# A convolution's first stage in three products of column halves, with its intermediate laid out for runs of 4 KB

## The chip, the cores and the metric

The kernel runs on one core of one Trainium2 chip. The metric is the device time of one execution in microseconds (us), the median of several runs. A core has TensorE (PE; PEld is its loading of weights), VectorE (DVE), ScalarE (ACT), GpSimd (POOL) and SyncE (SP), which issues nearly all transfers here. The data move on 16 DMA engines that all transfers share.

## What is computed

The reference is a long convolution by FFT, followed by a "soft" mixture of experts over the convolution's rows, all in float32:

```
x (8, 5696, 128), h (5696, 128)
y = irfft(rfft(x, 2S) * rfft(h, 2S))[:, :S]          # causal convolution along the sequence
t = y.reshape(45568, 128)
logits = t @ phi                                     # phi (128, 32): 8 experts x 4 slots
slots  = softmax(logits, over tokens).T @ t          # (32, 128)
out    = softmax(logits, over slots) @ expert_mlp(slots)    # 1024 hidden units, relu
```

The convolution is done as a transform of 90 x 64 points (`N1 = 90`, `N2 = 64`; 89 rows of 64 tokens hold the 5696 tokens), forward for `h` and the eight batches of `x`, a product with `h`'s transform, and back.

## The kernel before

The work is software-pipelined by hand: a loop over steps `t` issues a piece of each stage, and the order of the instructions on each engine's queue is the order in which the loop writes them. There are 72 steps with a first stage (`NA = 72`: `h` and eight batches, eight chunks each), then ten steps without it (`without_a`), then a tail.

**First stage, one chunk a step.** `load_x(c)` (L178) loads 89 rows into one of three buffers, as a transfer of 80 rows and one of 9. `fold(c, comp)` (L195) makes, on POOL, the sum (`comp` 0) and the difference (`comp` 1) of two mirrored column blocks, 128 x 512 each, into `xf[comp]`. `stage_a(c, comp)` (L204) multiplies one fold by two 128-column tables (L211), evacuates each product on ACT (L213) into `fst`, and stores the useful rows into the DRAM tensor `fd[g]` of shape (2, 64, 45, 2, 128): half of the frequencies `a`, position `n2`, frequency `q`, part `c`, channel. Each store has 45 rows and four runs of 1 KB in a row (L217). There are two a call, four a chunk. `stage_a(t, 0)` opens a step and `stage_a(t, 1)` stands after `stage_c5`, in the step's later half.

**Second stage, three units a step (23 a batch).** `load_g(u)` (L224) loads two frequencies of all 128 pairs (a, n2) as one run of 2 KB per row (L230), four units ahead, into five buffers `gt`. `stage_b1` multiplies (L244, PSUM tile `bt`) and applies `h`'s transform on DVE (L265, L268, L270). `stage_b2` multiplies again (L284), evacuates into `zst` on ACT (L288) and stores it into the DRAM tensor `zd` (L289). A step has three places for this, `slot_b`. It begins at `t = 9` (`LAG_B`). The group `g = 0`, the transform of `h`, only fills tables.

**Third stage and the mixture, one pair of chunks in two steps,** from `t = 27` (`LAG_C`), with loads two steps ahead. `load_pair` (L308) loads from `zd` into the one buffer `zc` in two transfers, of 64 and of 26 rows of 16 KB. `stage_c1` multiplies (L336: each product is two matmuls of 64 columns whose results stand in the two halves of a PSUM bank), `after` (L353) adds on DVE (L341, L342) and POOL (L359). `stage_c2` to `stage_c6`, `softmax` and `dispatch` transpose, take logits and exponentials, and accumulate the slots. `stage_c6` stores the token softmax into DRAM (`c_t`).

**The tail** computes the last batch's third stage, joins the four partial maxima (`join_quarters`), runs the experts and writes the output (L860 to L877). The last store (L875) has 128 rows in SBUF that go to 8 batches x 16 rows in DRAM.

SP issues the transfers in program order, and one that waits holds up all behind it.

Of the kernel before, what the change touches and what calls it, by code (L numbers as in the profile page):

```python
# [10 lines left out]
F32 = mybir.dt.float32  # L11
AF = mybir.ActivationFunctionType
AL = mybir.AluOpType
# [6 lines left out]
    return [(0, 64, 32), (64, n - 64, 0)]  # L20


def transform_tables(S, N1, N2, CH, X0, F0, F1):

    N, R1, HALF, P = N1 * N2, S // N2, N2 // 2, 2 * N2
    k1 = np.arange(N1)
    alpha = np.pi * (k1 + 0.5) / N1
    m1 = np.arange(R1) - (N1 - 1) / 2
    a1 = np.outer(m1, alpha)  # L40
    s1 = np.stack([np.cos(a1), -np.sin(a1), -np.cos(a1)], 1)
    a0 = np.outer(alpha, np.arange(N1 // 2) + 0.5)
    i1 = np.stack([np.cos(a0), -np.sin(a0), -np.cos(a0)], 1)
    NP = N1 // 2
    part = s1
    s1 = np.zeros((P, 3, P))
    for a, p in enumerate((F0, F1)):
        s1[X0:X0 + R1, :, p:p + NP] = part[:, :, a * NP:(a + 1) * NP]
    part = i1[np.arange(N1).reshape(2, NP).T.reshape(-1)]
    i1 = np.zeros((P, 3, N2))  # L50
    for r, n, p in z_blocks(N1):
        i1[p:p + n, :, 0:NP] = part[r:r + n]
    k2 = np.arange(N2)
    omega = np.pi * (k1[:, None] + 2 * N1 * k2[None] + 0.5) / N
    m2 = np.arange(HALF) - (N2 - 1) / 2
    a2 = m2[None, :, None] * omega[:, None, :]
    w = np.concatenate([np.cos(a2), np.sin(a2)], 1)
    back = np.arange(N2).reshape(2, HALF // CH, CH).transpose(1, 0, 2).reshape(-1)
    NU = (NP + 1) // 2
    turn = (N1 - 1) / 2 * alpha[:, None] + (N2 - 1) / 2 * omega  # L60
    wq = np.zeros((2, N2, NP, N2))
    vq = np.zeros((2, N2, NU, 2, N2))
    tn = np.zeros((2, N2, 2, NU, 2))
    for a in range(2):
        wq[a] = w[a * NP:(a + 1) * NP].transpose(1, 0, 2)
        for q in range(NP):
            vq[q % 2, :, q // 2, a] = w[a * NP + q][back].T
            tn[q % 2, :, 0, q // 2, a] = np.cos(turn[a * NP + q]) / N
            tn[q % 2, :, 1, q // 2, a] = np.sin(turn[a * NP + q]) / N
    wq, vq, tn = [t.reshape(P, *t.shape[2:]) for t in (wq, vq, tn)]  # L70
    return [np.ascontiguousarray(t, dtype=np.float32) for t in (s1, i1, wq, vq, tn)]
# [3 lines left out]
def kernel(  # L75
# [33 lines left out]
    CH = 4  # L109
# [6 lines left out]
    NQ = NJ // 2  # L116
    assert S == R1 * N2 and R1 == N1 - 1 and D == P and CH == Q == 4
    SPLIT = R1 // 16 * 16
    X0, F0, F1 = 20, 6, 82
    ctx.enter_context(tc.manual_schedule())  # L120

    t_s1, t_i1, t_w, t_v, t_turn = [
        nc.inline_tensor(t, f"tab_{n}").ap()
        for n, t in zip(("s1", "i1", "w", "v", "turn"), transform_tables(S, N1, N2, CH, X0, F0, F1))]
    fd = [nc.dram_tensor(f"f_{g}", (2, N2, NP, 2, D), F32, kind="Internal").ap() for g in range(B + 1)]
    zd = [nc.dram_tensor(f"z_{b}", (NP, 2 * N2, 2, D), F32, kind="Internal").ap() for b in range(B)]
    cd = nc.dram_tensor("c_t", (P, B * NQ, Q, 2, MH), F32, kind="Internal").ap()

# [28 lines left out]
    apool = lead.enter_context(tc.tile_pool(name="apool", bufs=2, side="right"))  # L157
    bpool = front.enter_context(tc.tile_pool(name="bpool", bufs=1))

    s1 = apool.tile([P, 3, P], F32, name="s1", tag="s1", bufs=1)  # L160
    wt = fconst.tile([P, NP, HP], F32, name="wt")
    vt = fconst.tile([P, NU, 2, HP], F32, name="vt")
    turn = fconst.tile([P, 2, NU, 2], F32, name="turn")
# [6 lines left out]


    xs = {}
    xf = [apool.tile([P, CH, D], F32, name=f"x{i}", tag=f"x{i}", bufs=1) for i in range(2)]
    xcs = [apool.tile([P, 2, CH, D], F32, name=f"xc{i}", tag=f"xc{i}", bufs=1) for i in range(3)]
    for t_ in xcs:
        nc.vector.memset(t_[:, :, :, :], 0.0)
# [18 lines left out]
    def fold(c, comp):  # L195
        if c not in xs:
            return
        t_ = xs.pop(c) if comp else xs[c]
        y_ = xf[comp]
        nc.gpsimd.tensor_tensor(out=y_[:, :, :], in0=t_[:, 0, :, :], in1=t_[:, 1, ::-1, :],  # L200
                                op=AL.subtract if comp else AL.add)
        folded[(c, comp)] = y_

    def stage_a(c, comp):  # L204
        g, j = divmod(c, NJ)
        src = folded.pop((c, comp))
        tab = (0, 1) if comp == 0 else (1, 2)
        st = apool.tile([P, CH, 2, D], F32, name="fst", tag="fst", bufs=3)
        for G in range(2):
            p = bank()  # L210
            nc.tensor.matmul(p[:, :], s1[:, tab[G], :],  # L211
                             src[:, :, :].rearrange("p n d -> p (n d)"), start=True, stop=True)
            nc.scalar.activation(st[:, :, G, :],  # L213
                                 p[:, :].rearrange("p (n d) -> p n d", d=D), AF.Copy)
        n0 = comp * HALF + CH * j
        for a, p in enumerate((F0, F1)):
            nc.sync.dma_start(  # L217
                out=fd[g][a, n0:n0 + CH, :, :, :].rearrange("n q c d -> q n (c d)"),
                in_=st[p:p + NP, :, :, :].rearrange("k n c d -> k n (c d)"))


    gs, prods = {}, {}
# [1 line left out]
    def load_g(u):  # L224
        if u >= (B + 1) * NU:
            return
        g, i = divmod(u, NU)
        n = min(2, NP - 2 * i)
        t_ = bpool.tile([P, 2, 2, D], F32, name="gt", tag="gt", bufs=5)
        nc.sync.dma_start(  # L230
            out=t_[:, 0:n, :, :].rearrange("p q c d -> p (q c d)"),
            in_=fd[g].rearrange("a r q c d -> (a r) (q c d)")[:, 4 * i * D:(4 * i + 2 * n) * D])
        gs[u] = t_

    def stage_b1(u, adder=nc.vector):
# [88 lines left out]
    def stage_c1(T):  # L324
# [27 lines left out]

        def after(a_):  # L353
            fold_out(a_, om[:, :, :], op[:, :, :])

            def additions():
                for v, o_, eng in ((1, op, nc.gpsimd), (0, om, nc.vector if tail else nc.gpsimd)):
                    for part_, sign in ((part(v, 1), AL.subtract), (part(v, 0), AL.add)):
                        eng.tensor_tensor(out=part_, in0=part(v, 0), in1=o_[:, :, :], op=sign)  # L359
            return additions  # L360

        ys[T] = y_
        return second
# [140 lines left out]
    def join_quarters():  # L504
# [5 lines left out]
        nc.vector.tensor_reduce(out=lr[:, 0, :], in_=p[0:1, 0:P].rearrange("p (k s) -> p s k", k=Q),  # L510
                                axis=AX.X, op=AL.min)
        nc.vector.tensor_copy(out=lr[:, 1:Q, :], in_=lr[:, 0:1, :].broadcast_to([1, Q - 1, NSL]))

        def spread():
            p = bank()
            nc.tensor.matmul(p[:, 0:1], lr[:, :, :].rearrange("p k s -> p (k s)"), one[:, :],
                             start=True, stop=True)
            le = tail["last"].tile([P, 1], F32, name="le")
            nc.vector.tensor_tensor(out=le[:, :], in0=p[:, 0:1], in1=low[:, 1:2], op=AL.subtract)
            nc.scalar.activation(le[:, :], le[:, :], AF.Exp)  # L520
            once = tail["last"].tile([P, NSL], F32, name="once")
            nc.vector.tensor_scalar(out=once[:, :], in0=rep4[:, 0, :], scalar1=le[:, 0:1],
                                    scalar2=None, op0=AL.mult)
            tail["once"] = once
        return spread


    LAG_B, LAG_C = NJ + 1, 3 * NJ + 3
# [13 lines left out]
    loaded = 0  # L542

    load_x(0)
    nc.scalar.dma_start(out=s1[:, :, :], in_=t_s1)
    for c in range(1, 3):
        load_x(c)
    nc.sync.dma_start(out=wt[:, :, :], in_=t_w)
# [8 lines left out]
    for t in range(last_front + 1):  # L557
# [35 lines left out]
        def without_a():  # L593
# [7 lines left out]
            if T is not None:  # L601
# [4 lines left out]
                    add(kept_[0])  # L606
                slot_around(middle, nc.gpsimd)
                load_pair(pair(-2))
                additions = kept_[1]()
                slot_around(lambda: stage_c5(U), nc.gpsimd)  # L610
                additions()
                softmax(U)
                return
            if t == last_front:
                load_pair(V + 2, (0,))
            slot_around(lambda: dispatch(pair(3)), nc.vector)
            slot_around(lambda: stage_c2(V, (3, 2)), nc.vector)
            slot_around(lambda: stage_c2(V, (1, 0)), nc.gpsimd)
            assert t < last_front or not (us or wait_b2)
            if t == last_front:  # L620
# [17 lines left out]
        if t >= NA:  # L638
            without_a()
            continue  # L640
        stage_a(t, 0)
        fold(t + 1, 0)
        if t == NA - 1:
            stage_a(t, 1)
        if pair(3) is not None:
            dispatch(pair(3))
        slot_b()
# [10 lines left out]
        if pair(5) is not None:  # L658
            stage_c6(pair(5))
        slot_b()  # L660
        if pair(-2) is not None:
            load_pair(pair(-2))
        load_x(t + 3)
        if t == NJ:
            prefetch(AHEAD)
        if after:
            after()()
        if U is not None:
            stage_c5(U)
        if t < NA - 1:  # L670
            stage_a(t, 1)
            fold(t + 1, 1)
        if pair(1) is not None:
            stage_c3(pair(1))
        slot_b()
# [19 lines left out]

    second = stage_c1(T)
    stage_c4(T - 1)
    second()()()
    stage_c5(T - 1)
    softmax(T - 1)  # L700
    nc.gpsimd.memset(y_[:, :, D:D + 1], 1.0)
# [20 lines left out]
    for V in range(T, NT - 1):  # L722
# [11 lines left out]
        if N < NT:  # L734
# [1 line left out]
            stage_c4(V)  # L736
            after = second()
            load_pair(N + 2)
            after()()
        else:  # L740
            stage_c2(V + 1)
            stage_c6(V - 1)
            stage_c4(V)
            stage_c3(V + 1)
            column_max(V + 1)
        if T < V and N < NT:
            placed_c()
        stage_c5(V)
        if N == NT:
            stage_c4(V + 1)  # L750
            join = join_quarters()
            dispatch(V)
            join()
            placed_c(False)
        softmax(V)
        if V == T:
            ybufs.insert(0, y_)
            stage_c1(T + 2)()()()
            load_pair(T + 4)
            nc.sync.dma_start(out=w1s[1][:, :, :],  # L760
                              in_=moe_w1[E // 2:].rearrange("e d f -> d e f"))
        else:
            for i in range(4 * (V - T - 1), min(4 * (V - T), E), 2):
                nc.sync.dma_start(
                    out=w2s[:, i:i + 2, :, :],
                    in_=moe_w2[i:i + 2].rearrange("e (p c) d -> p e c d", p=P))
    stage_c5(NT - 1)
    dispatch(NT - 1)
    placed_c()
    softmax(NT - 1)  # L770
    placed_c(False)
    assert list(Ls) == [NT - 2, NT - 1] and not (ys or ds or prods or gs or zs or xs or folded or wait_b2
                or kept)
# [135 lines left out]
```

## Time and profile before

| | before |
|---|---|
| three runs, median (range) | 926.88 us (922.38 to 935.1) |
| the profiled execution, its own time | 935.1 us |
| its span, from the first to the last instruction | 933.3 us |
| busy: PE / DVE / ACT / POOL | 842.3 / 664.2 / 511.5 / 469.6 us |
| moved by DMA | 273.04 MB in 172239 packets |
| queue q1 (SP's), share of 16 engines' span | 90.9% |
| TensorE's mean granted clock | 0.949 |

Lengths of steps, as the distance between the starts of successive steps' first L211 matmul:

| steps | what runs beside the first stage | us a step |
|---|---|---|
| 1 to 6 | nothing | 3.5 to 5 |
| 11 to 15 | second stage of `h` | 6.8 |
| 18 to 24 | second stage | 8.3 |
| 27 to 71 | second and third stage | 11.15, mean of the usual pair |

The last store of the first stage is issued by SP at 693 us. A transfer is cut into packets, one for each contiguous run; each packet record has a size and a duration. The median durations by size are 46 ns (1 KB), 61 (1440 B), 84 (2 KB), 159 (4 KB) and 716 (16 KB), 36 for 768 B and 22 for 368 B. Each DMA engine that takes part in a transfer ends its share with a packet of 4 bytes, 9 ns, that reports to the semaphore.

In a line of the groups stand: line, engine, operation, output <- inputs, shape, count | busy time, mean ns of one | idle time of the engine just before them and what ended most of it. A float32 matmul is two records. In a line of windows stand the stretch, its length, then busy time and count of PE, PEld, DVE, ACT and POOL, the granted clock, the mean busy share of the 16 DMA engines, and GB/s. A line of waits has: engine and line, what ended the wait, us in total, times, longest.

### The profile page before, as it was taken

How to read it: one execution, taken by the hardware profiler on the slowest of the kernel's cores; microseconds unless marked ns; L12 is line 12 of the kernel's file. 1: busy time of each engine (PE TensorE's matmuls, PEld its weight loads, DVE VectorE, ACT ScalarE, POOL GpSimd, SP SyncE). 2: the span in 40 equal slices, each digit the busy share in tenths (PEclk: the TensorE clock that was granted, in tenths of full speed). 3: DMA queues.
4: the chain of work that ended last, by engine and by line, in shares of the span. 5: the costliest groups of instructions: out<-in, count | busy, mean ns of one | idle time of the engine just before them, and what ended most of it. 6: DMA issues, size and time to landing. Idle time of an engine off the chain costs nothing. (4 is left out here: it accounts for less than half of the span.)

```text
span 933.3 us, 20359 instructions
## 1 busy us (share of the span) xinstructions
PE 842.3 (90%) x7220; PEld 402.3 (43%) x7220; DVE 664.2 (71%) x1127; ACT 511.5 (55%) x1016; POOL 469.6 (50%) x431
## 2 busy tenths in 40 slices
PE   6978788899999999999999999989998888996893
PEld 2323233334444444444444444434443434453793
DVE  3035576678878877888888788858878886795542
ACT  3556544455656655666666566646664444574442
POOL 4647623245555555555555555545545665468000
PEclk9989999999999999999999999989999988998956
DMA  9999899999999989999999999989979886675798
GB/s 296 272 270 277 264 325 316 295 306 318 284 296 311 332 262 298 321 328 279 291 308 333 280 310 309 308 270 307 319 258 279 288 269 230 218 273 196 272 405 327
DMA packets 172239, 273.04 MB, mean 293 GB/s; under 512 B 14742, under 2 KB 117398, under 8 KB 168965
## 3 DMA queue, kind: packets, MB, share of 16 engines
q1 hardware_dynamic: 171563, 271.38, 90.9%
q8 instruction: 58, 0.95, 0.4%
q10 hardware_dynamic: 576, 0.36, 0.2%
q14 instruction: 42, 0.34, 0.1%
HBM read 142.85 MB, written 128.21 MB: 290 GB/s over the span
## 5 line engine op out<-in xcount | busy, mean ns | idle before, releaser
L211 PE MATMUL bank<-x,s 128*128 128x512 f32 x576 | 284.3, 621 | 9.9 <-POOL x L200 8.0
L200 POOL TENSOR_TENSOR x<-xc 128x512 f32<-128x512 f32 x144 | 183.7, 1277 | 144.9 <-PE bank L211 90.8
L213 ACT ACTIVATE fst<-bank 128x512 f32<-128x512 f32 x288 | 167.7, 597 | 91.7 <-PE bank L211 63.6
L265 DVE TENSOR_TENSOR pr<-bt,Hr 128x512 f32<-128x512 f32 (+1 forms) x184 | 126.6, 688 | 100.1 <-PE bt L244 97.1
L288 ACT ACTIVATE zst<-bz 128x512 f32<-128x512 f32 (+1 forms) x184 | 108.2, 588 | 153.7 <-PE bz L284 147.8
L244 PE MATMUL bt<-gt,wt 64*64 64x256 f32 x1620 | 140.1, 409 | 45.8 <-DMA gt<-f 16.1
L211 PEld LDWEIGHTS bank<-x,s 128*128 128x128 f32 x576 | 100.1, 192 | 133.2 <-issue 88.8
L270 DVE TENSOR_TENSOR yf<-pr,pi 128x512 f32<-128x512 f32 (+1 forms) x169 | 145.2, 859 | 5.8
L268 DVE TENSOR_TENSOR pi<-bt,Hi 128x512 f32<-128x512 f32 (+1 forms) x184 | 125.0, 679 | 0.0
L284 PE MATMUL bz<-yf,vt 64*64 64x256 f32 x1440 | 118.7, 389 | 2.2 <-ACT yt L371 0.5
L244 PEld LDWEIGHTS bt<-gt,wt 64*64 64x64 f32 x1620 | 45.4, 133 | 163.1 <-PE bank L211 45.3
L336 PE MATMUL bank<-zc,i 128*64 128x512 f32 x448 | 112.9, 628 | 0.0
L359 POOL TENSOR_TENSOR y<-y,op 128x512 f32<-128x512 f32 x64 | 77.5, 1211 | 60.3 <-DVE op L341 57.7
L359 POOL TENSOR_TENSOR y<-y,om 128x512 f32<-128x512 f32 x54 | 75.9, 1405 | 2.1
L284 PEld LDWEIGHTS bz<-yf,vt 64*64 64x64 f32 x1440 | 53.2, 134 | 37.8 <-issue 12.8
L255 DVE SCALAR_TENSOR_TENSOR Hr<-bt,turn,ph 128x128 f32<-128x128 f32 (+1 forms) x46 | 16.0, 348 | 68.9 <-ACT ph L253 68.9
L371 ACT ACTIVATE yt<-bank 128x360 f32<-128x360 f32 x128 | 51.9, 472 | 15.8 <-PE bank L369 15.6
L369 PE MATMUL bank<-ident,y 109*128 109x109 f32 x512 | 58.9, 268 | 1.0 <-DVE y L359 0.7
L415 POOL MEMSET dt<- 64x8 f32 x32 | 3.4, 107 | 109.3 <-ACT dn L418 87.0
L369 PEld LDWEIGHTS bank<-ident,y 109*128 109x128 f32 x512 | 50.5, 145 | 16.6 <-issue 10.8
L860 PE MATMUL op<-so,cT 32*128 32x128 f32 x704 | 44.9, 376 | 6.2 <-ACT o L869 5.8
L336 PEld LDWEIGHTS bank<-zc,i 128*64 128x64 f32 x448 | 28.1, 140 | 51.4 <-issue 46.3
(100 smaller groups left out, 910.1 us busy)
## 6 DMA issues: line engine op xcount, KB each, us to landing
f<-fst SPq DMA_DIRECT2D x288, 180.0 KB
gt<-f SPq DMA_DIRECT2D x198, 256.0 KB
z<-zst SPq DMA_DIRECT2D x176, 256.0 KB
zc<-z SPq DMA_DIRECT2D x28, 1024.0 KB
xc<-in_x_dram SPq DMA_DIRECT2D x64, 320.0 KB
out_dram<-o SPq DMA_DIRECT2D x15, 1024.0 KB
zc<-z SPq DMA_DIRECT2D x28, 416.0 KB
out_dram<-o SPq DMA_DIRECT2D x9, 768.0 KB
```

The costliest lines, as they stand in the source:

```text
L200: nc.gpsimd.tensor_tensor(out=y_[:, :, :], in0=t_[:, 0, :, :], in1=t_[:, 1, ::-1, :], op=AL.subtract if comp else AL.add)
L211: nc.tensor.matmul(p[:, :], s1[:, tab[G], :], src[:, :, :].rearrange("p n d -> p (n d)"), start=True, stop=True)
L213: nc.scalar.activation(st[:, :, G, :], p[:, :].rearrange("p (n d) -> p n d", d=D), AF.Copy)
L244: nc.tensor.matmul(bt[q * HP:(q + 1) * HP, a, 0:2 * D], wt[r, 2 * i + q, :], t_[r, q, :, :].rearrange("p c d -> p (c d)"), start=True, sto ...
L265: nc.vector.tensor_tensor(out=pr[r, :, :, :], in0=pv, in1=Hr[r, i, :, :].unsqueeze(2).broadcast_to([n * HP, 2, 2, D]), op=AL.mult)
L268: nc.vector.tensor_tensor(out=pi[r, :, :, :], in0=pv, in1=Hi[r, i, :, :, :], op=AL.mult)
L270: adder.tensor_tensor(out=y_[r, :, :, :], in0=pr[r, :, :, :], in1=pi[r, :, ::-1, :], op=AL.add)
L284: nc.tensor.matmul(bz[a * HP:(a + 1) * HP, q, 0:2 * D], vt[r, i, a, :], y_[r, a, :, :].rearrange("p c d -> p (c d)"), start=True, stop=True)
L288: nc.scalar.activation(st[:, 0:n, :], bz[:, 0:n, 0:2 * D], AF.Copy)
L336: nc.tensor.matmul(p[h_ * HP:(h_ + 1) * HP, :], i1[:, tab, :], t_[:, h_, o, :, q, :], start=True, stop=True)
L359: eng.tensor_tensor(out=part_, in0=part(v, 0), in1=o_[:, :, :], op=sign)
L369: nc.tensor.transpose(p[:, i * TR:(i + 1) * TR], ys[T][0:TR, k * CH + i, 0:D], ident[0:TR, 0:TR])
```

## The change

The two folds of a chunk go through the first stage together. Per chunk there are three products instead of four. Each is two matmuls of 64 columns, one per fold (`h_`), into the two halves of a PSUM bank. Products 0 and 1 hold the frequencies `q < 32` of both halves `a` (a row is h, q, a), product 2 holds the remaining 13 frequencies (52 rows for each fold). Products 0 and 1 are evacuated into one tile of 128 rows x 4 KB, which is stored as one transfer; product 2 is stored as two transfers of 52 rows with runs of 2 KB. In DRAM `n2` now lies inside `q` and `a`: `fd` is (32, 2, 64, 2, 128) and the rest `fr` is (13, 2, 2, 64, 128). The second stage loads two runs of 1 KB per row where `q < 32`, and runs of 512 bytes in the rest. The early call `stage_a(t, False)` makes products 0 and 1. The late one makes product 2 and issues all three stores; it and the second fold of the next chunk move ahead of `load_pair`, `load_x` and `after`. The folds rotate through three buffers.

The diff also takes back an ordering of other parts: in `without_a` the additions of `after` come ahead of `stage_c5` again, one adder goes from POOL to DVE and one the other way, and in the tail `placed_c`, `column_max`, `stage_c4`, `stage_c6`, `join_quarters` and `softmax` change places.

```diff
-    fd = [nc.dram_tensor(f"f_{g}", (2, N2, NP, 2, D), F32, kind="Internal").ap() for g in range(B + 1)]
+    fd = [nc.dram_tensor(f"f_{g}", (NP2, 2, N2, 2, D), F32, kind="Internal").ap() for g in range(B + 1)]
+    fr = [nc.dram_tensor(f"fr_{g}", (NP - NP2, 2, 2, N2, D), F32, kind="Internal").ap()
+          for g in range(B + 1)]
...
-    def stage_a(c, comp):
+    stored = {}
+
+    def stage_a(c, late):
         g, j = divmod(c, NJ)
-        src = folded.pop((c, comp))
-        tab = (0, 1) if comp == 0 else (1, 2)
-        st = apool.tile([P, CH, 2, D], F32, name="fst", tag="fst", bufs=3)
-        for G in range(2):
+        src = [folded[(c, h_)][:, :, :].rearrange("p n d -> p (n d)") for h_ in range(2)]
+        if late:
+            rest = apool.tile([P, CH, D], F32, name="fsr", tag="fsr")
+            dst = [(2, rest[:, :, :])]
+        else:
+            stored[c] = st = apool.tile([P, CH, 2, D], F32, name="fst", tag="fst")
+            dst = [(G, st[:, :, G, :]) for G in range(2)]
+        for G, d_ in dst:
             p = bank()
-            nc.tensor.matmul(p[:, :], s1[:, tab[G], :],
-                             src[:, :, :].rearrange("p n d -> p (n d)"), start=True, stop=True)
-            nc.scalar.activation(st[:, :, G, :],
-                                 p[:, :].rearrange("p (n d) -> p n d", d=D), AF.Copy)
-        n0 = comp * HALF + CH * j
-        for a, p in enumerate((F0, F1)):
+            for h_ in range(2):
+                nc.tensor.matmul(p[h_ * HP:(h_ + 1) * HP, :], s1[:, h_, G, :], src[h_],
+                                 start=True, stop=True)
+            nc.scalar.activation(d_, p[:, :].rearrange("p (n d) -> p n d", d=D), AF.Copy)
+        if not late:
+            return
+        for h_ in range(2):
+            del folded[(c, h_)]
+        n0 = CH * j
+        nc.sync.dma_start(
+            out=fd[g].rearrange("q a (h j n) c d -> j h (q a) (n c d)", h=2, n=CH)[j],
+            in_=stored.pop(c)[:, :, :, :].rearrange("p n c d -> p (n c d)"))
+        for h_ in range(2):
             nc.sync.dma_start(
-                out=fd[g][a, n0:n0 + CH, :, :, :].rearrange("n q c d -> q n (c d)"),
-                in_=st[p:p + NP, :, :, :].rearrange("k n c d -> k n (c d)"))
+                out=fr[g][:, :, :, h_ * HALF + n0:h_ * HALF + n0 + CH, :].rearrange(
+                    "q c a n d -> (q c a) (n d)"),
+                in_=rest[h_ * HP:h_ * HP + 4 * (NP - NP2), :, :].rearrange("k n d -> k (n d)"))
...
-        nc.sync.dma_start(
-            out=t_[:, 0:n, :, :].rearrange("p q c d -> p (q c d)"),
-            in_=fd[g].rearrange("a r q c d -> (a r) (q c d)")[:, 4 * i * D:(4 * i + 2 * n) * D])
+        q0 = 2 * i
+        if q0 < NP2:
+            nc.sync.dma_start(
+                out=t_[:, 0:n, :, :].rearrange("p q c d -> p q (c d)"),
+                in_=fd[g].rearrange("q a r c d -> (a r) q (c d)")[:, q0:q0 + n, :])
+        else:
+            q0 -= NP2
+            nc.sync.dma_start(
+                out=t_[:, 0:n, :, :].rearrange("p q c d -> p (q c) d"),
+                in_=fr[g].rearrange("q c a r d -> (a r) (q c) d")[:, 2 * q0:2 * (q0 + n), :])
...
-                additions = kept_[1]()
-                slot_around(lambda: stage_c5(U), nc.gpsimd)
-                additions()
+                kept_[1]()
+                slot_around(lambda: stage_c5(U), nc.vector)
...
-        stage_a(t, 0)
+        stage_a(t, False)
         fold(t + 1, 0)
...
         slot_b()
+        if t < NA - 1:
+            stage_a(t, True)
+            fold(t + 1, 1)
         if pair(-2) is not None:
             load_pair(pair(-2))
         load_x(t + 3)
...
         if after:
-            after()()
+            after()
         if U is not None:
             stage_c5(U)
-        if t < NA - 1:
-            stage_a(t, 1)
-            fold(t + 1, 1)
```

## The prediction, made before the changed kernel ran

> **What bounds the kernel now.** I read the page's slices first, then two steps of the middle by windows, then the transfers by issue, then the end of the trace, and last the groups and the queue's waits.
>
> The slices, each 23.3 us; digits are tenths busy:
>
> ```profile
> PE   6978788899999999999999999989998888996893
> ACT  3556544455656655666666566646664444574442
> DMA  9999899999999989999999999989979886675798
> ```
>
> The DMA engines are full from the first slice until the first stage ends at about slice 30, TensorE from about slice 9. Two neighbouring steps of the middle (start to start of L211 groups, 22.3 us, so 11.15 us a step):
>
> ```profile
> core 0: us, PE busy (x) PEld busy (x) DVE busy (x) ACT busy (x) POOL busy (x), PEclk, DMA share, GB/s
> 404.50:426.80 22.30, 22.30 (x200) 10.44 (x196) 19.18 (x32) 13.96 (x27) 12.79 (x12) 1.00 0.99 316
> ```
>
> TensorE has no gap, and the mean share of the 16 DMA engines is 0.99. Both are at their end, so a change that lightens only one moves little, and one that loads the fullest DMA engine lengthens the step.
>
> How evenly a transfer loads the engines therefore matters. The issues on SP's queue:
>
> ```profile
> f<-fst SPq DMA_DIRECT2D x288, 180.0 KB
> gt<-f SPq DMA_DIRECT2D x198, 256.0 KB
> out_dram<-o SPq DMA_DIRECT2D x2, 256.0 KB
> ```
>
> Each engine that takes part in a transfer ends its share with a packet of 4 bytes, and the trace has 14,422 of these on q1. That number can be decoded. Suppose a transfer runs on the largest number up to 16 that divides the outermost count on both of its sides. The 288 stores of 45 rows take 15 engines, the 207 gt loads and 184 z stores (128 rows) 16, the 32 zc loads of 64 rows 16 and the 32 of 26 rows 13, the x loads of 80 and of 9 rows (72 each) 16 and 9, c_t and cl (25 and 7) 16, the two copies into zd 16 and 6, 11 loads of weights and tables 16, and 25 output stores 16. That is 14,414. One is left: the last store (L875), 128 rows in SBUF, in DRAM 8 (batch) by 16. By 8 engines it adds 8: 14,422 exactly; by 16 it would be 14,430. The end of the trace, where only stores run:
>
> ```profile
> 926.00:928.00 2.00, 0.00 (x0) 0.00 (x0) 0.00 (x0) 0.00 (x0) 0.00 (x0) 0.50 1.00 385
> 928.00:929.00 1.00, 0.00 (x0) 0.00 (x0) 0.00 (x0) 0.00 (x0) 0.00 (x0) 0.50 0.69 266
> 930.40:931.60 1.20, 0.00 (x0) 0.00 (x0) 0.00 (x0) 0.00 (x0) 0.00 (x0) 0.50 0.07 26
> ```
>
> The last 1.2 us are one engine alone (0.07 is one of 16), at 26 GB/s: in the packet records it is 16 packets of 2 KB, 80 ns apart, 128 rows over 8. An outermost count of 8 did confine that transfer to 8 engines.
>
> **The change, part by part.** *The store of the first stage.* The new fd store has 128 rows in SBUF, but in DRAM its dimensions are h (2), q a (64), 4 KB; h is outermost, with the smaller stride, so it cannot merge. The count of the decoded rule is 2: two engines carry 512 KB. At 26 GB/s each that is 262,144 B / 26 = 10.1 us; by packets, 64 of 4 KB at a median of 159 ns (loads; stores of 1 and 2 KB cost as loads do) is 10.2. It replaces, on engine 0, four shares of 12 packets at 46 ns, 2.2 us. The two fr stores have 52 rows merged into one count, 13 engines, 4 packets each at 84 ns: 0.7 us. If it ran on 16 engines the fd store would be 8 x 159 = 1.3 us.
>
> *The loads of gt.* Before, each engine took 2.9 units x 8 packets of 2 KB a step, 1.9 us. After, 16 of a batch's 23 units have runs of 1 KB, two units a step with 16 packets each on every engine: 2 x 16 x 46 = 1.5. The other seven have runs of 512 B, 26 packets a step. No packet of 512 B stands in the trace; 368 B take 22 ns, 768 B 36, so 27 is between: 0.7 us. Together 2.2 us, +0.3.
>
> *Engine 0 in a full step*, in us: fd store 10.2, fr 0.7, gt 2.2, z 45 x 46 = 2.1, zc three 16 KB at 716 = 2.1, x 12 x 84 = 1.0, c_t 4 x 61 = 0.2, endings 0.1: 18.6. Without zc and c_t (t 17 to 24) 16.2, without z (t 9 to 16) 14.1, fd, fr and x alone (t 0 to 8) 11.9. The same count for the kernel before gives 9.7 where 11.15 is measured, because packets are slower when all engines run.
>
> *TensorE.* L211's two passes of a 128-column product cost 0.98 us. L336 already has the new form, two 64-column products side by side:
>
> ```profile
> L211 PE MATMUL bank<-x,s 128*128 128x512 f32 x576 | 284.3, 621 | 9.9 <-POOL x L200 8.0
> L336 PE MATMUL bank<-zc,i 128*64 128x512 f32 x448 | 112.9, 628 | 0.0
> L213 ACT ACTIVATE fst<-bank 128x512 f32<-128x512 f32 x288 | 167.7, 597 | 91.7 <-PE bank L211 63.6
> ```
>
> In the two steps above L336's 4 pairs take 3.87 us, 0.97 a pair, so the halves overlap. Three pairs instead of four products save 1.0 us a step of TensorE, and three evacuations instead of four 0.6 us of ScalarE. Six weight loads of 64 columns replace four of 128 (137 against 192 ns). All this is hidden here: beside 18.6 us TensorE's 10.1 is no bound. Folds stay two per chunk (1277 ns); a third buffer lets the first run early. Hidden.
>
> *SP's queue.* One store fewer per chunk saves about 0.4 us of issue (median 412 ns). The stores, load_pair, load_x and the additions swap places within a step; the x chunk still has two steps before its fold, which covers it. More weighty is what waits behind the slow store. Eight completion semaphores are used in turn, and a transfer is issued after the one eight before it has landed:
>
> ```profile
> SPq L217 <- DMA zc<-z: 99.9, 39, 4.7
> ```
>
> That is the eighth transfer after each zc load. Now the eighth after each fd store waits some 10 us: z stores and gt loads, and for those bt. Meanwhile seven transfers are queued behind it on engine 0, 3.9 us of work on odd steps, 6.7 on even. The landing and five issues of about 0.45 us fit beside them, so I cost this at nothing; without that cover it is up to 1 us a step, 71 us.
>
> *The other edits.* In the ten steps without first stage the additions go ahead of stage_c5 again, an adder moves between POOL and DVE (1279 against 860 ns) and c2's goes the other way; in the tail placements and column_max move. None is measured. No step should move by more than one addition (1.4 us, either way) and the tail by more than four copies of 0.97: bounds -18 and +18, I take 0.
>
> *The sum.* First store issued at about 13 us, 7 us of tables on the engine, 71 intervals (9 x 11.9 + 8 x 14.1 + 8 x 16.2 + 46 x 18.6 = 1205), the last store 10, and what followed the last f store before: 933.3 - 693 = 240. Span 1475. The execution profiled took 935.1, 8 over the median, so against the median some 5 to 10 less; but contention, not counted above, adds about as much. I stay at 1475.
>
> Bounds: packets start 4 ns sooner than their durations say (80 for 84), which makes a full step 17.6 and takes 60 off; with 18 of the other edits, 1400. All packets but the fd store's slowed by 15%, as now: 19.9 a full step, 75 more, 1550. TensorE granted 0.50, as the rows above show when it idles, would need 20.2 a step, still near that; the 1 us of gaps adds 71.
>
> **A rule of the Trainium skill, weighed.** The row: 256 KB on 8 engines left the last at 26 GB/s. The page "DMA: Bandwidth & Descriptors", section "Rules for kernel authors", advises to coalesce small transfers into one of 128 partitions, which speaks for this change, and the 341 GB/s that the page's section "Bandwidth" states for 1 MB would give, as an estimate, 1.5 us for the store and a kernel near 910 us. The same section limits a transfer to the count of its outermost dimension when that is below 16, which would give the sum above. I take the second because the count of packets decides it; no run shows the first here.
>
> **Rivals.**
> *Faster: sixteen engines, TensorE sets the step.* If the hardware deals the 128 SBUF rows regardless of h, engine 0 has 9.7 us of packets as before, and TensorE's 1.0 us could come off 45 saturated steps (t from 27), 45 us; the DMA share of 0.97 to 0.99 leaves 0.3 of it, 15 us: 912 by that, 882 at most. The deciding point is eight engines: 16 x 159 = 2.5 us, the time of the old stores. Against it: 14,422.
> *Same: sixteen engines, DMA sets the step.* gt's short runs (+0.3 us x 63 steps) eat the wider stores' gain: 927, 915 to 945. For it: DMA share 0.99. Against it, the same count.
> *Slower still: two engines and gaps.* The queue runs dry after each fd store, or TensorE falls to half clock: 1550 to 1650. For it: SP already waits 99.9 us at L217. Against: seven queued transfers.
>
> **How the numbers follow.** Two engines, fed: 0.80, 1475, own range 1390 to 1560. Two engines with gaps: 0.11. Sixteen, TensorE: 0.05. Sixteen, DMA: 0.04. The range takes in half of the gap case and 0.75 of the 0.80: 1380 to 1600. Faster by over 2% is 0.05, within 2% (about what can be told from no change) 0.04, slower 0.91.
>
> **What would show it.** Right: steps of about 12 us at the start and 18 to 19 in the middle; DMA share about 0.25, then 0.5; 200 GB/s or less; TensorE near 6 tenths; fd's transfer landing 10 us or more after its issue; two 4-byte packets per fd store. Products at 0.97 us a pair, L213's successors at 597 ns x216. Wrong: DMA share still 0.9 with the fd store landing within 3 us, then a rival of sixteen engines holds.

## The result, and the profile after

| | before | after |
|---|---|---|
| median (range) | 928.11 us (922.38 to 935.1) | 1428.13 us (1425.59 to 1433.55) |
| ratio, 95% interval | | 1.539 (1.527 to 1.551) |
| span of the profiled execution | 933.3 | 1431.8 |
| packets of 4 bytes on q1 | 14,422 | 12,118 |
| a full step (mean of steps 27 to 68, between first-stage stores) | 11.27 | 17.96 |
| from the first store of the last chunk to the end | 242.7 | 255.7 |

The change costs 500 us. Times of kernels that ran four times or more are given from here on as medians of their fast runs (at most 1.5% over the kernel's fastest), and ratios with their 95% intervals compare fast runs alone. The slices of the changed kernel, each 35.8 us:

```profile
PE   4444555655566666666666666666666665889785
...
PEclk8767986677778888888888888888888887999785
DMA  5224334544565556565656565656665656977579
GB/s 181 95 99 150 131 122 149 183 161 162 178 191 187 192 183 195 188 196 183 196 188 197 184 197 184 200 184 196 190 196 184 197 171 192 305 229 250 203 300 358
```

Both rows that were full are half empty up to slice 33, where the first stage ends: as means over engines, nothing is busy. The mean hides where the load is. One early step, cut into stretches, and below it two full steps, show it:

```profile
core 0: us, PE busy (x) PEld busy (x) DVE busy (x) ACT busy (x) POOL busy (x), PEclk, DMA share, GB/s
50.80:53.00 2.20, 0.20 (x1) 0.20 (x2) 0.00 (x0) 0.47 (x1) 1.52 (x2) 0.50 0.53 186
53.00:55.00 2.00, 2.00 (x5) 0.67 (x6) 0.00 (x0) 0.00 (x0) 0.96 (x1) 0.50 0.13 53
55.00:57.00 2.00, 2.00 (x7) 1.07 (x5) 0.00 (x0) 0.00 (x0) 0.00 (x0) 0.50 0.12 51
...
668.50:704.80 36.30, 24.09 (x204) 10.99 (x204) 18.91 (x31) 12.71 (x25) 13.58 (x12) 0.83 0.60 194
```

A share of 0.13 is 2 of 16, and 53 GB/s is twice the 26 of one engine. In these stretches two engines carry the store while fourteen have nothing. In q1's packet records of 700 to 1100 us exactly two packets are in flight 28% of the time, and fewer than two 0.1% of it: the two engines do not idle. What waits for it, first on SP's queue, then on ACT:

```profile
SPq L319 <- DMA f<-fst: 287.3, 48, 8.6
SPq L255 <- DMA f<-fst: 66.8, 8, 10.3
```

```profile
L227 PE MATMUL bank<-x,s 128*64 128x512 f32 x864 | 272.4, 677 | 70.4 <-POOL x L209 70.4
...
L229 ACT ACTIVATE fst<-bank 128x512 f32<-128x512 f32 x144 | 78.9, 595 | 323.5 <-DMA f<-fst 307.6
```

L319 is the z store, held up by the semaphore's turn; L255 is the gt load, held up eight times, once each for eight of the nine groups (`h` and the batches), until the group's last fd store has landed. L229 waits for the buffer that the slow store still reads. The evacuations are as cheap as forecast (595 ns), and nobody profits.

### The profile page after: what moved, and what is told of

Read it like the earlier page. It is cut to its first block, busy times and chain, and to the rows that moved or that the text cites. A ratio compares the mean times of both kernels' runs of the same rounds, so it can differ in the third digit from the quotient of the medians.

```text
span 1431.8 us, 20624 instructions
## 1 busy us (share of the span) xinstructions
PE 914.5 (64%) x7508; PEld 414.6 (29%) x7508; DVE 658.6 (46%) x1127; ACT 470.9 (33%) x946; POOL 479.3 (33%) x429
## 4 chain that ended last, share of the span: by engine, by line
DMA 65%; PE 20%; SPq 4%; DVE 4%; issue 3%; POOL 2%; ACT 2%; DVEq 0%; POOLq 0%; ACTq 0%
DMA f<-fst 22%; DMA gt<-f 21%; DMA xc<-in_x_dram 12%; PE bank L366 5%; PE bt L274 3%; DMA gt<-fr 3%; PE bz L314 2%; DMA zc<-z 2%; PE bank L227 2%; PE bank L396 2%; DMA out_dram<-o 2%; SPq L197 1%; SPq L239 1%; PE op L882 1%; PE bank L481 1%
## 5 line engine op out<-in xcount | busy, mean ns | idle before, releaser
L274 PE MATMUL bt<-gt,wt 64*64 64x256 f32 x1620 | 164.6, 477 | 412.2 <-DMA gt<-f 282.0
L209 POOL TENSOR_TENSOR x<-xc 128x512 f32<-128x512 f32 x144 | 203.1, 1413 | 588.4 <-DMA xc<-in_x_dram 393.1
L227 PE MATMUL bank<-x,s 128*64 128x512 f32 x864 | 272.4, 677 | 70.4 <-POOL x L209 70.4
L274 PEld LDWEIGHTS bt<-gt,wt 64*64 64x64 f32 x1620 | 52.7, 153 | 535.5 <-issue 381.2
L229 ACT ACTIVATE fst<-bank 128x512 f32<-128x512 f32 x144 | 78.9, 595 | 323.5 <-DMA f<-fst 307.6
L366 PE MATMUL bank<-zc,i 128*64 128x512 f32 x448 | 140.5, 761 | 0.0
L227 PEld LDWEIGHTS bank<-x,s 128*64 128x64 f32 x864 | 80.6, 149 | 195.8 <-POOL x L209 101.0
L314 PE MATMUL bz<-yf,vt 64*64 64x256 f32 x1440 | 136.0, 439 | 1.5 <-ACT yt L398 0.6
L314 PEld LDWEIGHTS bz<-yf,vt 64*64 64x64 f32 x1440 | 61.9, 153 | 45.1 <-issue 18.7
L229 ACT ACTIVATE fsr<-bank 128x512 f32<-128x512 f32 x72 | 43.1, 598 | 29.5 <-PE bank L227 28.2
```

The source lines that it names most:

```text
L227: nc.tensor.matmul(p[h_ * HP:(h_ + 1) * HP, :], s1[:, h_, G, :], src[h_], start=True, stop=True)
L229: nc.scalar.activation(d_, p[:, :].rearrange("p (n d) -> p n d", d=D), AF.Copy)
L274: nc.tensor.matmul(bt[q * HP:(q + 1) * HP, a, 0:2 * D], wt[r, 2 * i + q, :], t_[r, q, :, :].rearrange("p c d -> p (c d)"), start=True, sto ...
L314: nc.tensor.matmul(bz[a * HP:(a + 1) * HP, q, 0:2 * D], vt[r, i, a, :], y_[r, a, :, :].rearrange("p c d -> p (c d)"), start=True, stop=True)
L366: nc.tensor.matmul(p[h_ * HP:(h_ + 1) * HP, :], i1[:, tab, :], t_[:, h_, o, :, q, :], start=True, stop=True)
```

## The experiments

The theory: two engines carry the fd store. The rivals: its layout in DRAM, the short loads, or the order in the step is what costs. Line numbers in fences are those of each kernel.

**Two stores of 64 rows (sixteen engines each).**

```diff
-        nc.sync.dma_start(
-            out=fd[g].rearrange("q a (h j n) c d -> j h (q a) (n c d)", h=2, n=CH)[j],
-            in_=stored.pop(c)[:, :, :, :].rearrange("p n c d -> p (n c d)"))
+        st = stored.pop(c)
+        for h_ in range(2):
+            nc.sync.dma_start(
+                out=fd[g].rearrange("q a (h j n) c d -> j h (q a) (n c d)", h=2, n=CH)[j, h_],
+                in_=st[h_ * HP:(h_ + 1) * HP, :, :, :].rearrange("p n c d -> p (n c d)"))
```

> The changed kernel with one edit: the fd store is two transfers of 64 rows, one per fold, so that its outermost count in DRAM is 64 and no longer 2. Bytes, runs of 4 KB, layout and loads stay. Theory (two engines carried the store): engine 0 has 8 x 159 ns = 1.3 us of it in place of 10.2, a full step falls from 18.0 us to 10.6 to 11.2, the time to 905 to 945. Rival (the layout in DRAM, the short runs of the loads, or the order of the step made it slow): the time stays above 1350. A third store changes SP's queue by one issue of about 0.5 us a step, hidden.

Measured: 979.9 us, from runs of 974.0 and 985.85; 1.053 of before (1.040 to 1.066). Of the 500 us, 448 are the two engines. But some 50 are left, more than the theory allowed: in the profiled execution, of 991.6 us, steps 10 to 14 last 9.7 us instead of 6.8, full steps 11.95 instead of 11.27.

**The same with fewer engines.** fd in four, eight or sixteen blocks, with 4 KB between them, so that a store's 64 rows cannot merge and its outermost count is that number.

```diff
-    fd = [nc.dram_tensor(f"f_{g}", (NP2, 2, N2, 2, D), F32, kind="Internal").ap() for g in range(B + 1)]
+    NB, PAD = 4, 1024
+    QB = NP2 // NB
+    FB = QB * 2 * N2 * 2 * D
+    fd = [nc.dram_tensor(f"f_{g}", (NB, FB + PAD), F32, kind="Internal").ap() for g in range(B + 1)]
...
-                out=fd[g].rearrange("q a (h j n) c d -> j h (q a) (n c d)", h=2, n=CH)[j, h_],
+                out=fd[g][:, 0:FB].rearrange("b (m h j e) -> j h b m e", m=QB * 2, h=2, j=NJ)[j, h_],
...
-                in_=fd[g].rearrange("q a r c d -> (a r) q (c d)")[:, q0:q0 + n, :])
+                in_=fd[g][q0 // QB, 0:FB].rearrange("(q m e) -> m q e", q=QB, e=2 * D)[:, q0 % QB:q0 % QB + n, :])
```

> As the run with two stores of 64 rows, but fd lies in four blocks with a gap of 4 KB between them, so that each store's outermost count is 4 and cannot merge; runs, bytes and everything else stay. Theory (the outermost count sets the number of engines): 2 x 16 packets of 159 ns = 5.1 us a step on each of four engines, a full step of 18.0 - 10.2 + 5.1 = 12.9 us, and by the steps 1070 to 1130 us. Rival (only the count 2 is special, or the time came from the layout): the time of the two stores of 64 rows, or that of the changed kernel.

> As the run with fd in four blocks, but with eight, so each fd store runs on eight engines. Theory (the fullest engine sets the step, and beside full traffic one of its 4 KB packets costs about 200 ns, as the runs with two stores of 64 rows on sixteen and on four engines show: 10 us + 0.2 us per packet a step): 16 packets a step on the fullest engine, a full step of 13.2 us, the time 1050 to 1100 us. Rival (the prediction's deciding point of eight engines, at 159 ns a packet and with the slack of the idle engines): a full step of 11.8 us as with sixteen, 985 to 1010 us.

> As the runs with fd in four and in eight blocks, but in sixteen: the same gaps of 4 KB in DRAM, and 64 rows as 16 by 4, so each fd store runs on sixteen engines. Theory (the number of engines made those two runs slow, not the gaps): as the two stores without gaps, 989 within 974 to 1005, full step 11.8 us. Rival (the gaps or the split layout cost time): above 1020.

| engines | packets of 4 KB a step on the fullest | full step in the trace, us | time, us (16 without gaps and 2: medians; the others: one run) |
|---|---|---|---|
| 16, no gaps | 8 | 11.95 | 979.9 |
| 16, gaps | 8 | 11.42 | 971.24 |
| 8, gaps | 16 | 12.91 | 1053.93 |
| 4, gaps | 32 | 16.18 | 1267.25 |
| 2, the changed kernel | 64 | 17.96 | 1428.13 |

The number of engines sets the time, and the gaps cost nothing measurable (the run with sixteen blocks came out 3 us under its range, a single run). The decoded rule holds beyond the kernel it was read from: with 15 engines for each old store replaced by 13 for each fr store and 2, 4, 8 or 16 for each fd store it gives 12,118, 12,550, 13,126 and 14,278 packets of 4 bytes, and the traces of the changed kernel and of the runs on four, eight and sixteen (without gaps) hold exactly these. My expectation for four engines missed by 140 us: it priced packets at their median, 159 ns, though between 400 and 650 us of that trace the 4 KB packets average 199 ns, those of 2 KB 136 instead of 84, those of 16 KB 934 instead of 716. On the fullest engine's 32, 12 and 3 packets this is some 2.5 of the 3.3 us that the full step missed by, an estimate. The price of 0.2 us per packet that I then took from these runs gave 1050 to 1100 us for eight, and 1053.93 came. It is a price beside traffic on all sixteen engines: with two it would make 10 + 64 x 0.2 = 22.8 us, and 17.96 came.

**First and second stage alone, with two stores; and the other edits alone.** The hunks of the diff were applied in part: in one kernel those of the first and second stage, in the other those of `without_a` and the tail.

> The kernel before with the new first and second stage alone (products, layout, loads, place in the step) and the fd store as two transfers of 64 rows; additions, adders and tail in the order of before. Against the run with two stores in the changed kernel it shows what the order of the other parts is worth: theory, at most 18 us either way, likeliest under 5. Against before it shows what three products and longer runs are worth once the store is on sixteen engines. Theory that TensorE sets the step: about 885 to 912. Theory that DMA sets it: 915 to 945.

> The kernel before with the other edits alone: additions ahead of stage_c5 again, the two adders exchanged, and the changed order of the tail; first stage, stores and loads as before. Theory: these edits are worth at most 18 us, 928 within 910 to 946, no part of the 500. Rival: a part of the loss is theirs, over 960.

Measured: 985.28 us (1.059, 1.048 to 1.069) and 938.79 (1.009, 1.004 to 1.014). The other edits cost some 8 us. The first stage alone keeps the loss, 55 us, and neither sum of mine for sixteen engines holds: something else in the first stage costs time.

**What else: the place of the second fold.** In the run with two stores, the chain that ended last between 66 and 90 us (steps with `h`'s transform; start, length, what):

```profile
72.57 3.21 PE bank L227 x6
75.78 1.01 PE bt L276 x8
...
76.86 0.48 ACT ph L285
...
77.37 0.35 DVE Hr L287
...
81.00 0.85 POOL Hi L293
81.85 1.24 POOL x L209
...
83.14 3.53 PE bank L227 x6
```

There is no DMA in it. A product now needs both folds of its chunk, and the second fold (L209) is queued on POOL behind the sign change of `Hi` (L293), which waits for the second stage, which waits for the products: from one L227 to the next 10.6 us. In full steps another wait stands out. TensorE's waits for the second stage's loads between 300 and 690 us, before and with two stores:

```profile
PE bt L244 <- DMA gt<-f: 7.3, 7, 2.9
```

```profile
PE bt L276 <- DMA gt<-f: 18.5, 9, 3.4
PE bt L276 <- DMA gt<-fr: 13.5, 4, 4.3
```

There TensorE's matmuls wait 32.0 us for loads instead of 7.3, and for a fold only its weight loads wait, 4.6 us. I moved the late call, with the stores that it issues, and both folds up:

```diff
         stage_a(t, False)
+        stage_a(t, True)
         fold(t + 1, 0)
-        if t == NA - 1:
-            stage_a(t, True)
+        fold(t + 1, 1)
...
-        if t < NA - 1:
-            stage_a(t, True)
-            fold(t + 1, 1)
```

> The changed kernel with the fd store as two transfers of 64 rows and, beside that, the late call of stage_a moved up to the early one, and both folds of the next chunk right behind it, so that the second fold no longer stands on POOL behind the second stage's work. Theory (in steps 9 to 16 a chain TensorE, ACT, DVE, POOL, fold, TensorE of 10.6 us sets the step because the second fold is queued behind the sign change of Hi): steps 9 to 16 fall from 9.5 to 7 to 8 us, 12 to 20 us off the time of the kernel with two stores; full steps stay, as DMA sets them. Rival (these steps are long because of the transfers): no change.

Measured: 953.24 us (1.027, 1.014 to 1.040), 27 us less. Steps 10 to 14 fall from 9.7 to 7.15: there the chain through the fold is shown. The full steps fall too, from 11.95 to 11.21, which I had not expected: TensorE's waits for the second stage's loads shrink from 32.0 to 9.3 us. The edit moved products, stores and folds together, and which of them brought the loads earlier is not shown. Steps 18 to 22 grow from 8.1 to 10.1: in these five steps TensorE now waits 4.3 us for DVE's `yf`, and with the product late not at all.

**Is it TensorE or DMA that sets the step of before?** Once with a product more, once with one less.

```diff
-            nc.tensor.matmul(p[:, :], s1[:, tab[G], :],
-                             src[:, :, :].rearrange("p n d -> p (n d)"), start=True, stop=True)
+            for _ in range(1 + (comp == 0 and G == 0)):
+                nc.tensor.matmul(p[:, :], s1[:, tab[G], :],
+                                 src[:, :, :].rearrange("p n d -> p (n d)"), start=True, stop=True)
```

> The kernel before with one of the four products of a chunk computed twice into the same bank, 0.98 us more of TensorE in every step and nothing else. Theory (DMA sets the step of the kernel before, TensorE's full row is a matter of how its time is recorded, and one product fewer is worth nothing): within 10 us of before, 928 to 940. Rival (TensorE sets it): about 45 us more in the 45 full steps, 960 to 985.

```diff
-            p = bank()
-            nc.tensor.matmul(p[:, :], s1[:, tab[G], :],
-                             src[:, :, :].rearrange("p n d -> p (n d)"), start=True, stop=True)
+            if not (comp == 1 and G == 1):
+                p = bank()
+                nc.tensor.matmul(p[:, :], s1[:, tab[G], :],
+                                 src[:, :, :].rearrange("p n d -> p (n d)"), start=True, stop=True)
```

> The kernel before with the second product of the difference fold left out (both halves of that fold's store are evacuated from the first product), so 0.98 us less of TensorE a step; evacuations, stores, loads and order as before. The output is not the reference's. A fifth product cost 42 us, so TensorE does set the step. Theory (TensorE and DMA end together, DMA share 0.97 to 0.99): most of the 45 us is lost, 915 to 928. Rival (TensorE alone sets it): 880 to 895.

Measured: with five products 972.87 us (1.047, 1.039 to 1.054), with three 926.68 (0.999, 0.995 to 1.003). My theory that TensorE's full row is only a matter of recording fell: one microsecond more costs 42 us. The full step grows by 0.58 of the 0.98 us, from 11.27 to 11.85, and steps 18 to 22 by 0.87, from 8.33 to 9.20, so TensorE was close to its end before and not quite at it. One product less brings nothing measurable, and the windows say why. Before, five products, three products, each over 330 us of full steps (PE, PEld, DVE, ACT and POOL busy, clock, DMA share, GB/s):

```profile
320.00:650.00 330.00, 323.07 (x2713) 148.53 (x2713) 267.75 (x436) 197.89 (x386) 182.12 (x157) 0.98 0.97 302
```

```profile
320.00:650.00 330.00, 330.00 (x2697) 152.81 (x2698) 258.48 (x423) 192.03 (x372) 177.37 (x153) 1.00 0.91 287
```

```profile
320.00:650.00 330.00, 308.25 (x2687) 137.29 (x2686) 279.12 (x440) 195.36 (x389) 189.10 (x159) 0.98 0.98 305
```

With five products TensorE is at 330 of 330 and the DMA share falls to 0.91. With three, TensorE has 22 us of room while the DMA share stays at 0.98 and the step at 11.27 us, as before. Two limits meet, and saving on TensorE alone buys nothing.

**The loads in runs of 1 KB, alone in the kernel before.**

```diff
-    fd = [nc.dram_tensor(f"f_{g}", (2, N2, NP, 2, D), F32, kind="Internal").ap() for g in range(B + 1)]
+    fd = [nc.dram_tensor(f"f_{g}", (2, N2, NP, 2 * D + 64), F32, kind="Internal").ap() for g in range(B + 1)]
...
-            out=t_[:, 0:n, :, :].rearrange("p q c d -> p (q c d)"),
-            in_=fd[g].rearrange("a r q c d -> (a r) (q c d)")[:, 4 * i * D:(4 * i + 2 * n) * D])
+            out=t_[:, 0:n, :, :].rearrange("p q c d -> p q (c d)"),
+            in_=fd[g].rearrange("a r q e -> (a r) q e")[:, 2 * i:2 * i + n, 0:2 * D])
...
```

> The kernel before with a gap of 256 bytes behind every 1 KB of fd, so that the second stage's loads come as two runs of 1 KB in place of one of 2 KB; stores, products and order as before. By packets: 23 a step at 84 ns become 46 at 46 ns on each engine, 0.2 us, so 10 to 20 us over the 63 steps if DMA sets them; 0 if TensorE does.

Measured: 935.5 us, 1.005 (1.0004 to 1.0096), about 5 us: under the sum by packets, barely above nothing.

**The best mixture.** Order of the other parts as before, two stores, products and folds early except in steps 17 to 26.

```diff
         stage_a(t, False)
-        fold(t + 1, 0)
-        if t == NA - 1:
+        early = not LAG_B + NJ <= t < LAG_C or t == NA - 1
+        if early:
             stage_a(t, True)
+        fold(t + 1, 0)
+        if early:
+            fold(t + 1, 1)
...
-        if t < NA - 1:
+        if not early:
             stage_a(t, True)
             fold(t + 1, 1)
```

> The kernel before with the new first and second stage, the fd store as two transfers of 64 rows, and additions, adders and tail in the order of before; the late call of stage_a and both folds stand behind the early call in all steps but 17 to 26, where they stand late as in the changed kernel. Theory (what kept the version with early products over before is 12 us in steps 17 to 24 and some 8 of the order of the other parts): 930 to 940, not faster than before, because DMA carries 0.3 us a step more. Rival (TensorE's saving comes through): under 915.

> The mixed version with its first product computed twice, 0.97 us more of TensorE a step, which gives the saving of the three products back. Theory (DMA sets the step once there are three products): within 10 us of the mixed version. Rival (TensorE still sets it): 35 to 45 us more.

Measured: 936.9 us (1.010, 1.005 to 1.015), and 984.00 (1.057, 1.051 to 1.064) with the product computed twice. Against the first and second stage alone, from which it differs only in the place of the late call and the folds, the mixed version saves 48 us. By the two traces 23 of them lie in steps 8 to 16 and 26 from step 26 to the end of the first stage; steps 18 to 22 are back at 8.0. It is not faster than before; no version here is. Its full step is 11.18 us at a DMA share of 0.99, about the old step. The rival came out for the doubled product: 47 us more. The windows of both kernels, full steps, the mixed version first:

```profile
320.00:650.00 330.00, 304.45 (x2936) 134.76 (x2934) 273.16 (x447) 185.38 (x366) 191.64 (x163) 1.00 0.99 306
```

```profile
320.00:650.00 330.00, 307.28 (x2832) 131.43 (x2824) 263.40 (x416) 173.98 (x341) 173.72 (x151) 1.00 0.93 285
```

With the doubled product the DMA share has dropped to 0.93, so DMA no longer sets this step, but TensorE is recorded busy for only 0.93 of it. With the work of four products it takes 11.89 us a step, where the old arrangement does four in 11.27. So the mixed arrangement leaves TensorE gaps, 22.7 us of the 330. More than half of that is a wait for DVE between the second stage's units:

```profile
PE bz L316 <- DVE yf L302: 12.6, 14, 1.6
```

That these gaps use up what the three products save is argued from this, and not shown by a run of its own.

## Why the prediction was right

**The engines.** The step that carried it, an outermost count of 2 in DRAM gives two engines, is shown three ways: the 4-byte packets, the share of 0.13 at 53 GB/s, and the series 2, 4, 8, 16. The section "Rules for kernel authors" of the Trainium skill's page "DMA: Bandwidth & Descriptors" gives advice both ways. Its limit by the outermost dimension agrees with these runs: an outermost 2 gave two engines. Its advice to coalesce does not hold here: the same rows in two transfers save 448 us.

**The sum.** 1475 us were forecast, 1428 came. The terms by stage (forecast, measured): steps 2 to 6 11.9 and 11.6, 10 to 13 14.1 and 13.7, 18 to 22 16.2 and 15.6, full 18.6 and 17.96. All are 0.3 to 0.6 too high. The mis-sized term is the packets' time, taken as whole durations: they start 4 ns sooner. The bound of 17.6 for that took off 1.0; the some 194 packets that the sum lists for engine 0 make 0.8, and 17.8. Contention was to add about as much as the 5 to 10 us by which the profiled execution lay above the median. The full step leaves 0.2 us for it (17.96 less 17.8, an estimate), 7 us in 46 full steps, so that held; with two engines at work the 4 KB packets averaged 164 ns between 400 and 650 us. Part of the error cancelled, and that is luck: the steps from 26 on took 797 us instead of 837, but step 8 lasted 25.6 us, not 11.9, since the first gt loads wait for the fd stores, and from the last fd store on it took 255.7 instead of 250.

**Cover.** "I cost this at nothing" for SP's queue held: 287.3 us of SP's waits, and the two engines still never ran dry (fewer than two packets in flight 0.1% of the time). The same paragraph's moves within the step were costed at nothing too, under the same cover. With the cover gone (sixteen engines), calling the products and folds early saves 27 us with the other edits in, and 48 in the mixed version. About half of the 48 lies in steps 8 to 16, by the second fold's place, which the prediction did not see: it counted the folds and not what stands ahead of them on POOL. The other half lies in the full steps, together with TensorE's waits for the second stage's loads, and its cause is open.

**TensorE.** That the saving is worth nothing here was right. A pair of half-width products costs about what one full product does: twelve records of three pairs took 2.80 us at full clock in the version with early products, 0.93 a pair beside 0.98.

**The rivals' numbers were wrong.** Sixteen engines were put at 912 or 927; two stores on sixteen gave 979.9. And "the deciding point is eight engines" failed: eight gave 1053.93. Measured one at a time, the place of the late call and the folds is worth 27 to 48 us, the other edits cost 8 and the short loads 5. With eight, the fd store's 4 KB packets cost 0.2 us beside full traffic (194 ns in that trace's mean from 450 to 650 us), not 159 ns, and the fullest engine's 16 are 8 more than with sixteen.

**The other edits** were bounded at 18 us either way and taken as 0; they cost about 8.

## What to carry to other kernels

Before merging transfers, write down the outermost count of each side's access pattern as issued and the largest number up to 16 that divides both: that gave the number of engines in every trace here. A 2 there cost 448 us, where the whole store was worth 2.2 us a step before. In a profile, a low mean DMA share beside long waits for one transfer can mean that few engines carry it; the share of a short stretch (0.13 is two of sixteen) tells it from a DMA that is idle. Where two engines of the chip are both full, test each with a little more and a little less before you pay for a saving on one; and when a product comes to need two inputs instead of one, look at what is queued ahead of the later one.

## What the runs showed of the hardware

A 4 KB packet has a median of 159 ns in all these kernels, but its mean between 400 and 650 us moves with the company: 164 ns in the changed kernel with its two engines, 216 in the kernel with two stores on sixteen, 164 again when the products are early. I had no price for 512 B; 27 ns, taken between 22 and 36, is the measured median. TensorE was granted 0.807 of its clock instead of 0.949, with 0.50 in the stretches of the early step above, and its busy time rose from 842.3 to 914.5 us though it did a product less in each step: beside long stalls, a lightened engine took longer.
